# Attention and a gated MLP on one core: where the layernorm of later token blocks is placed, and how fill matmuls are dealt out among the others

## The chip, the cores and the metric

The kernel runs on one core of one Trainium2 chip. The metric is device time in microseconds (us) for one execution; smaller is better. The core has five engines that run side by side and meet only through semaphores: TensorE (PE in the profile, with its weight loads as PEld), VectorE (DVE), ScalarE (ACT), GpSimd (POOL) and SyncE (SP), which issues most DMA transfers here. In this kernel the order of instructions on every engine is fixed by the order of the program's text: an instruction whose input is late holds up everything behind it on the same engine.

## The reference

One launch computes an attention branch `s`, a gate `g` from an MLP, and their product on a residual. All inputs are bf16.

```python
x = A_x                                   # 1 x 2048 x 512
xn = (x - mean) / sqrt(var + 1e-5)        # layernorm over the 512 columns
# attention: 32 query heads, 8 key/value heads, head width 128, the last W = 512 cached rows
q = (xn @ wq)                             # 2048 x 4096 -> 32 heads
p = softmax(q @ k.T * 128 ** -0.5)        # 2048 x 512 per head
s = concat_heads(p @ v) @ wo              # 2048 x 4096 @ 4096 x 512
# gate
g = silu(silu(xn @ w1) @ w2)              # 512 -> 1792 -> 512
out = x + s * g
```

## The kernel before

The 2048 tokens are cut into four blocks of 512 (`NBLK = 4`, `BLKT = 4` tiles of 128 tokens each). After a start-up stage that makes the first half of block 0's MLP, the main loop has 128 steps: one step for each block and query head (`HQ = 32`), so steps 0 to 31 are block 0, 32 to 63 block 1, and so on. A step issues twelve matmuls of its own: four scores, four that make the query two steps ahead, and four for the value product of four steps ago (`LAG = 4`). Between these it puts "fill" matmuls that belong elsewhere: in block 0 the MLP of all four blocks (392 of them), in the later blocks the output projection of the block before (four a step). Every matmul of the loop is 128x128 weights on 512 columns.

```python
LAG = 4
PS_BUFS = {"sc": 4, "q": 1, "o": 1, "f": 2}      # PSUM banks: 4 for scores, 1, 1, and 2 for fill

def stats(b, j):                                  # layernorm statistics of tile j of block b
    st = work.tile([P, nc.vector.BN_STATS_DIM], FP32, name="st", bufs=4)
    nc.vector.bn_stats(out=st, in_=x_blk[b][:, j, :])
    nc.vector.bn_aggr(out=mv[:, b * BLKT + j, :], in_=st)

def rstd_of(t0, n): ...                           # (var + 1e-5) ** -0.5 on GpSimd

def center(b, j):                                 # x <- (x - mean) * rstd, in place
    nc.vector.tensor_scalar(out=x_blk[b][:, j, :], in0=x_blk[b][:, j, :], ...)

def flip_x(b, j):                                 # transposed by DMA into xnT, which the matmuls read
    nc.sync.dma_start_transpose(xnT[b][:, :, j * P : (j + 1) * P], x_blk[b][:, j, :])
```

The fill of block 0 is made of two kinds of group. A hidden group (`h_unit`) is four matmuls into one fill bank, then a tanh on ACT and a multiply on DVE that empty the bank; one block has 14 of them. An output group (`o_unit`) is 14 matmuls into one bank, then the same two operations; one block has four. The order of the fill is: output groups of block 0, then hidden and output groups of block 1, of block 2, of block 3.

```python
def h_unit(f, c):
    if c == 0:
        cur["ps"] = ps.tile([P, BLK], FP32, name="h_ps", tag="f", bufs=2)
    nc.tensor.matmul(cur["ps"], w1_sb[f // FH][:, c, ...], xnT[b][:, c, 0:BLK], ...)
    if c == ND - 1:                               # ND = 4
        nc.scalar.activation(th, cur["ps"], ACT.Tanh, scale=0.5)
        nc.vector.scalar_tensor_tensor(out=hT[b][f // 2][:, f % 2, :], in0=th, scalar=1.0,
                                       in1=cur["ps"], op0=ALU.add, op1=ALU.mult)
```

Own work of a step: `score(s, j)` is one matmul into a score bank and an exponential on ACT; `normalise(s, j0, j1)` is a reciprocal and two multiplies on DVE; `flip(s)` is one DMA transpose of the step's 128x2048 probabilities, issued by SP; `q_units` and `pv_units` each end in a copy from PSUM on DVE (`qT`, `oT`).

The start: the loads, and the main loop with its hand-set cuts.

```python
for j in range(2):
    nc.sync.dma_start(x_blk[0][0:HP4, j, :], x0v[0:HP4, j, :])       # HP4 = 64 rows
    nc.scalar.dma_start(x_blk[0][HP4:P, j, :], x0v[HP4:P, j, :])
NE = NEARLY * P                                                       # 512 columns
nc.sync.dma_start(w1_sb[0][:, :, 0:NE], w1v[:, :, 0:NE])
nc.scalar.dma_start(x_blk[0][:, 2:4, :], x0v[:, 2:4, :])
nc.sync.dma_start(w1_sb[0][:, :, NE:], w1v[:, :, NE : FH * P])        # FH * P = 896 columns
nc.sync.dma_start(w1_sb[1], w1v[:, :, FH * P :])
nc.sync.dma_start(w2_sb[0], w2v[:, 0:FH, :])
load_x(1)
load_kq(0)
# ... w2_sb[1], further keys, queries' weights and values, load_x(2), load_x(3)

# start-up stage, block 0: statistics and centring of tiles 0 and 1, ten warm-up matmuls,
# transposes on PE, then 14 pairs of hidden groups, 256 columns at a time
for i in range(2 * FH):
    h_pair(i, i // FH)            # pair i: hidden columns f = 2*(i%7), 2*(i%7)+1; f >= 7 reads w1_sb[1]
    if i == 3:                    # transposes of tiles 2 and 3, and their copies to xnT[0] (ACT, DVE)
        ...
    # ... stats(1, .), and the queries of steps 0 and 1

def spread(n):
    cut = [n // 6] * 6
    for k in (5, 4, 1, 3, 0, 2)[: n % 6]:
        cut[k] += 1
    return cut if n != 4 else (0, 0, 0, 0, 2, 2)

for s in range(NSTEP):
    b, h = divmod(s, HQ)
    n = 4
    if b == 0:
        n = min(4 * (h + 1), n_more) + (h + 1) * (n_mlp - n_more) // HQ - done   # n_more = 16, n_mlp = 392
    cut = spread(n)
    qu = q_units(s + 2) if s + 2 < NSTEP else []
    pu = pv_units(s - LAG) if s >= LAG else []
    score(s, 0)
    if s >= 1:
        normalise(s - 1, 2, 3); flip(s - 1)
    for u in qu[:2]: u()
    pump(cut[0])                                  # pump(n): the next n fill matmuls
    for u in qu[2:]: u()
    pump(cut[1])
    score(s, 1)
    for u in pu[:2]: u()
    pump(cut[2])
    for u in pu[2:]: u()
    pump(cut[3])
    score(s, 2)
    normalise(s, 0, 1)
    pump(cut[4])
    score(s, 3)
    pump(cut[5])
    for b2, s0 in ((2, 2), (3, 8)):               # one tile's statistics a step: block 2 in 2 to 5, 3 in 8 to 11
        if s0 <= s < s0 + BLKT: stats(b2, s - s0)
        if s == s0 + BLKT - 1: rstd_of(b2 * BLKT, BLKT)
    if s < 2:
        for j in (2 * s, 2 * s + 1): center(1, j); flip_x(1, j)
    for b2, s0 in ((2, 7), (3, 14)):              # one tile centred and transposed a step: 7 to 10, 14 to 17
        if s0 <= s < s0 + BLKT: center(b2, s - s0); flip_x(b2, s - s0)
    # ... loads of later keys, values and weights
```

From step 27 on `wo` is loaded, and after the last step a tail multiplies block 3 out with fewer products; neither is touched.

Of the kernel before, what the change touches and what calls it, by code (L numbers as in the profile page):

```python
# [9 lines left out]
P = 128  # L10
# [6 lines left out]
LAG = 4  # L17
# [5 lines left out]
def kernel(  # L23
# [12 lines left out]
    nc = tc.nc  # L36
# [10 lines left out]
    BLKT = 4  # L47
# [3 lines left out]
    NSTEP = NBLK * HQ  # L51
    FH = NFC // 2
    HALF = BLK // 2
    HP = HQ // 2
    HP4 = P // 2
# [28 lines left out]
    w1_sb = [reg.tile([P, ND, FH * P], BF16, name=f"w1_{i}", tag=f"big{i}") for i in range(2)]  # L84
# [8 lines left out]
    x_blk = {}  # L93
# [13 lines left out]
    def stats(b, j):  # L107
# [4 lines that stand above are left out]
    def rstd_of(t0, n):  # L112
        v = rstd[:, t0 : t0 + n]
        nc.gpsimd.tensor_scalar_add(v, mv[:, t0 : t0 + n, 1], 1e-5)
        nc.gpsimd.tensor_tensor(out=v, in0=v, in1=neg_half[:, 0:n], op=ALU.pow)
# [5 lines left out]
    def center(b, j):  # L121
        t = b * BLKT + j
        nc.vector.tensor_scalar(
            out=x_blk[b][:, j, :],
            in0=x_blk[b][:, j, :],
            scalar1=mv[:, t, 0:1],
            scalar2=rstd[:, t : t + 1],
            op0=ALU.subtract,
            op1=ALU.mult,
        )  # L130

    def flip_x(b, j):
        nc.sync.dma_start_transpose(xnT[b][:, :, j * P : (j + 1) * P], x_blk[b][:, j, :])

    def load_kq(g):
        nc.sync.dma_start_transpose(
            kT[g].rearrange("p (o w) -> p o w", o=1), A_k_cache[0, g, ds(SK - W, W), :]
        )
        nc.sync.dma_start(wq_sb[g], wqv[:, :, g * REP * DH : (g + 1) * REP * DH])

    def load_v(g):
        nc.sync.dma_start(
            v_sb[g], A_v_cache[0, g, ds(SK - W, W), :].rearrange("(c p) d -> p c d", p=P)
        )
# [82 lines left out]
    def score(s, j):  # L227
        h = s % HQ
        if j == 0:
            p_all[s] = work.tile([P, NKC, BLKT, P], BF16, name="p_all", tag="p_all", bufs=4)  # L230
            den[s] = work.tile([P, BLKT], FP32, name="den", bufs=3)
        sc = ps.tile([P, W], FP32, name="sc_ps", tag="sc", bufs=4)
        nc.tensor.matmul(  # L233
            sc, qT[s][:, j * P : (j + 1) * P], kT[h // REP], start=True, stop=True
        )
        nc.scalar.activation(  # L236
            p_all[s][:, :, j, :],
            sc.rearrange("p (kc q) -> p kc q", q=P),
            ACT.Exp,
            scale=INV_SQRT_DH,  # L240
            accum_out=den[s][:, j : j + 1],
        )

    def normalise(s, j0, j1):
        rden = work.tile([P, 2], FP32, name="rden", bufs=4)
        nc.vector.reciprocal(rden, den[s][:, j0 : j1 + 1])  # L246
        for j in range(j0, j1 + 1):
            nc.vector.tensor_scalar_mul(  # L248
                p_all[s][:, :, j, :], p_all[s][:, :, j, :], rden[:, j - j0 : j - j0 + 1]
            )  # L250

    def flip(s):
        pT[s] = work.tile([P, NKC, BLK], BF16, name="pT", tag="pT", bufs=4)
        nc.sync.dma_start_transpose(
            pT[s].rearrange("p kc (j q) -> p (kc j) q", q=P), p_all[s][:, :, :, :]
        )
# [47 lines left out]
    def new_wo(tag):  # L304
        wo_tiles[tag] = reg.tile([P, len(WO_HOME[tag]), D], BF16, name=f"wo_{tag}", tag=tag)
# [20 lines left out]
    def out_units(b):  # L326
        acc = {}
        xes = {}

        def mm(j, h):  # L330
            t = b * BLKT + j
            if h == 0:
                acc[j] = ps.tile([P, D], FP32, name="s_ps", tag="f", bufs=2)
            nc.tensor.matmul(  # L334
                acc[j],
                oT[(b * HQ + h) // 2][:, h % 2, j * P : (j + 1) * P],
                wo_of(h),
                start=(h == 0),
                stop=(h == HQ - 1),
            )  # L340
            if h == HQ // 2:
                xes[j] = reg.tile([P, D], BF16, name="x_e", tag=f"pair{4 + j % 2}")
                nc.gpsimd.dma_start(xes[j], x2[ds(t * P, P), :])
            if h == HQ - 1:
                xe = xes[j]
                sg = reg.tile([P, D], FP32, name="sg", tag=f"pair{2 + j % 2}")
                nc.vector.tensor_tensor(out=sg, in0=acc[j], in1=g_sb[b][:, j, :], op=ALU.mult)
                nc.vector.scalar_tensor_tensor(
                    out=xe, in0=sg, scalar=0.25, in1=xe, op0=ALU.mult, op1=ALU.add
                )  # L350
                nc.gpsimd.dma_start(out2[ds(t * P, P), :], xe)  # L351

        return [lambda a=a: mm(*a) for a in out_order()]
# [254 lines left out]
    w1v = B_w1.rearrange("(c p) f -> p c f", p=P)  # L608
# [5 lines left out]
    with tc.manual_schedule(engines={ENG.PE, ENG.Activation, ENG.DVE, ENG.SP, ENG.Pool}):  # L614
        new_x(0)
        x0v = x2[ds(0, BLK), :].rearrange("(j p) d -> p j d", p=P)
        for j in range(2):
            nc.sync.dma_start(x_blk[0][0:HP4, j, :], x0v[0:HP4, j, :])  # L618
            nc.scalar.dma_start(x_blk[0][HP4:P, j, :], x0v[HP4:P, j, :])
        NE = NEARLY * P  # L620
        nc.sync.dma_start(w1_sb[0][:, :, 0:NE], w1v[:, :, 0:NE])
        nc.scalar.dma_start(x_blk[0][:, 2:4, :], x0v[:, 2:4, :])
        nc.sync.dma_start(w1_sb[0][:, :, NE:], w1v[:, :, NE : FH * P])
        nc.sync.dma_start(w1_sb[1], w1v[:, :, FH * P :])
        nc.sync.dma_start(w2_sb[0], w2v[:, 0:FH, :])
        load_x(1)
        load_kq(0)
# [82 lines left out]
        for i in range(2 * FH):  # L710
# [8 lines left out]
            if i in (2 * FH - 3, 2 * FH - 2):  # L719
                k = i - 2 * FH + 3  # L720
# [11 lines left out]
        def pump(n):  # L732
            nonlocal done
            for _ in range(n):
                if fill:
                    fill.pop(0)()
                    done += 1
# [11 lines left out]
        }  # L749
        sums = col_sums()  # L750

        def spread(n):

            cut = [n // 6] * 6
            for k in (5, 4, 1, 3, 0, 2)[: n % 6]:
                cut[k] += 1
            return cut if n != 4 else (0, 0, 0, 0, 2, 2)

        n_more = 4 * LAG
        wo_first = False  # L760
        for s in range(NSTEP):
            b, h = divmod(s, HQ)
            if b >= 1 and h == 0:
                assert done >= n_mlp or b > 1
                fill += out_units(b - 1)
            n = 4
            if b == 0:
                n = min(4 * (h + 1), n_more) + (h + 1) * (n_mlp - n_more) // HQ - done
            cut = spread(n)
            qu = q_units(s + 2) if s + 2 < NSTEP else []  # L770
            pu = pv_units(s - LAG) if s >= LAG else []
            score(s, 0)
            if s >= 1:
                normalise(s - 1, 2, 3)
                flip(s - 1)
            for u in qu[:2]:
                u()
            pump(cut[0])
            for u in qu[2:]:
                u()  # L780
            pump(cut[1])
            score(s, 1)
            for u in pu[:2]:
                u()
            pump(cut[2])
            for u in pu[2:]:
                u()
            pump(cut[3])
            score(s, 2)
            normalise(s, 0, 1)  # L790
            pump(cut[4])
            score(s, 3)
            if s == NSTEP - 1:
                normalise(s, 2, 3)
                flip(s)
            pump(cut[5])
            while sums and sums[0][0] <= s:
                sums.pop(0)[1]()
            for b2, s0 in ((2, 2), (3, 8)):
                if s0 <= s < s0 + BLKT:  # L800
                    stats(b2, s - s0)
                if s == s0 + BLKT - 1:
                    rstd_of(b2 * BLKT, BLKT)
            if s < 2:
                for j in (2 * s, 2 * s + 1):
                    center(1, j)
                    flip_x(1, j)
            for b2, s0 in ((2, 7), (3, 14)):
                if s0 <= s < s0 + BLKT:
                    center(b2, s - s0)  # L810
                    flip_x(b2, s - s0)
            if s % REP == 1 and s < HQ and s // REP + 2 < HKV:
                load_kq(s // REP + 2)
                load_v(s // REP + 2)
            if not wo_first and done >= n_mlp - BLKT * NFC:
                new_wo("big0")
                new_wo("big1")
                wo_first = True
            if s == HQ:
                for tag in ("big2", "big3", "pair0", "pair1"):  # L820
                    new_wo(tag)
            for args in wo_plan.get(s, []):
                load_wo(*args)
# [29 lines left out]
```

The softmax here doesn't subtract the row's maximum and nothing guards it: scores larger than these inputs give would overflow.

## Time and profile before

| | |
|---|---|
| device time, median of 3 | 551.11 us (550.99 to 552.62) |
| span of the profiled execution | 548.9 us |
| granted TensorE clock | 1.00 |
| PE matmul busy | 542.9 us (99%) in 2676 matmuls |
| DVE busy | 458.3 us (83%) |
| ACT busy | 390.2 us (71%) |
| mean DMA traffic | 163 GB/s |
| loop steps of block 0 (first score of step 0 to that of step 32) | 22.16 to 187.69 us |
| loop steps of blocks 1 to 3 | 187.69 to 514.89 us |

In the profile, a line of the timeline gives the start in us, the duration in us, the engine, the line of the kernel, the operation, what it writes and reads (`out<-in`) and how many instructions were merged; in square brackets the idle time of that engine before it and what ended it. A busy time of PE is not PE at its peak, because a matmul's record is longer than the distance to the next one: the recorded matmuls of the loop take 380 ns each, and start 216 ns apart when nothing holds them up.

### The profile page before, as it was taken

What the parts mean: (1) busy time and instruction counts of PE and PEld (TensorE: products, weight loads), DVE (VectorE), ACT (ScalarE), POOL (GpSimd) and SP (SyncE); (2) the same over time, 40 slices, a digit from 0 to 9 for tenths busy, and PEclk for the clock granted to TensorE, in tenths of its full rate; (3) what the DMA queues carried; (4) which work ended last, traced back from release to release, by engine and by line L of the source; (5) the groups of instructions that cost most, each with busy time, mean ns of one, the idle gap of its engine ahead of it and who ended that gap; (6) DMA issues with size and microseconds to landing.
All of it is one profiled execution on the core that took longest, in us unless ns stands there. A gap on an engine that the chain in (4) does not pass through costs nothing.

```text
span 548.9 us, 8539 instructions
## 1 busy us (share of the span) xinstructions
PE 542.9 (99%) x2676; PEld 260.9 (48%) x2676; DVE 458.3 (83%) x1262; ACT 390.2 (71%) x1125; POOL 20.4 (4%) x41
## 2 busy tenths in 40 slices
PE   8999999999999999999999999999999999999997
PEld 5644444444444444444444444444444444444586
DVE  6869987976886688898888888988889889988897
ACT  5558756766776677777777777777788888888700
POOL 1000000000000100010001000100010000100010
PEclk9999999999999999999999999999999999999999
DMA  8968778768749799979887988797889887988831
GB/s 273 264 112 181 154 149 165 152 145 170 148 87 184 174 205 229 200 161 185 162 143 159 188 158 150 153 192 153 154 155 183 154 154 153 193 153 154 152 99 39
DMA packets 297869, 89.69 MB, mean 163 GB/s; under 512 B 282336, under 2 KB 296928, under 8 KB 297824
## 3 DMA queue, kind: packets, MB, share of 16 engines
q1 hardware_dynamic: 296080, 85.09, 78.6%
q0 software_dynamic: 1312, 3.67, 2.6%
q10 hardware_dynamic: 432, 0.39, 0.3%
q8 instruction: 21, 0.34, 0.2%
q14 instruction: 24, 0.20, 0.1%
HBM read 17.30 MB, written 2.10 MB: 35 GB/s over the span
## 4 chain that ended last, share of the span: by engine, by line
PE 96%; DMA 1%; DVE 1%; SPq 0%; ACT 0%; issue 0%
PE o_ps L276 20%; PE q_ps L211 20%; PE sc_ps L233 20%; PE s_ps L334 15%; PE oB_ps L180 9%; PE h_ps L147 6%; PE m_ps L477 4%; PE h_ps L697 2%; DMA w_1_112<-in_B_w_dram 1%; ACT th L157 0%; SPq L618 0%; DVE hT_4_1763 L158 0%; DVE gate_419 L190 0%; DVE hT_5_1764 L158 0%; DVE hT_2_1761 L158 0%
## 5 line engine op out<-in xcount | busy, mean ns | idle before, releaser
L236 ACT ACTIVATE p_all<-sc_ps 128x512 bf16<-128x512 f32 x512 | 305.4, 597 | 103.3 <-PE sc_ps L233 101.2
L248 DVE TENSOR_SCALAR p_all<-p_all,rden 128x512 bf16<-128x512 bf16 x512 | 158.0, 351 | 9.1
L282 DVE CAST oT<-o_ps 128x512 bf16<-128x512 f32 x128 | 88.3, 690 | 40.5 <-PE o_ps L276 39.6
L236 ACT ACTIVATION_READ_ACCUMULATOR p_all<-sc_ps 128x1 f32 x512 | 100.7, 197 | 0.0
L233 PEld LDWEIGHTS <-qT 128*128 128x128 bf16 x512 | 50.1, 98 | 61.4 <-issue 1.4
L223 DVE CAST qT<-q_ps 128x512 bf16<-128x512 f32 x111 | 76.3, 687 | 1.6 <-PE q_ps L211 1.5
L334 PEld LDWEIGHTS <-oT 128*128 128x128 bf16 x384 | 37.5, 98 | 45.3
L246 DVE RECIPROCAL rden<-den 128x2 f32<-128x2 f32 x256 | 40.5, 158 | 10.8 <-ACT p_all L236 10.8
L157 ACT ACTIVATE th<-h_ps 128x512 bf16<-128x512 f32 x42 | 25.1, 598 | 9.1 <-PE h_ps L147 9.1
L334 PE MATMUL s_ps<-wo_big_2086,oT 128*128 128x512 bf16 x84 | 26.0, 380 | 0.0
L334 PE MATMUL s_ps<-wo_big_2348,oT 128*128 128x512 bf16 x84 | 26.0, 380 | 0.0
L334 PE MATMUL s_ps<-wo_big_2087,oT 128*128 128x512 bf16 x84 | 26.0, 380 | 0.0
L334 PE MATMUL s_ps<-wo_big_2347,oT 128*128 128x512 bf16 x84 | 26.0, 380 | 0.0
L233 PE MATMUL sc_ps<-kT_91,qT 128*128 128x512 bf16 x64 | 24.3, 380 | 0.0
L233 PE MATMUL sc_ps<-kT_92,qT 128*128 128x512 bf16 x64 | 24.3, 379 | 0.0
L233 PE MATMUL sc_ps<-kT_93,qT 128*128 128x512 bf16 x64 | 24.3, 379 | 0.0
L233 PE MATMUL sc_ps<-kT_94,qT 128*128 128x512 bf16 x64 | 24.3, 379 | 0.0
L233 PE MATMUL sc_ps<-kT_96,qT 128*128 128x512 bf16 x64 | 24.3, 379 | 0.0
L233 PE MATMUL sc_ps<-kT_97,qT 128*128 128x512 bf16 x64 | 24.3, 379 | 0.0
L233 PE MATMUL sc_ps<-kT_95,qT 128*128 128x512 bf16 x64 | 24.3, 379 | 0.0
L233 PE MATMUL sc_ps<-kT_98,qT 128*128 128x512 bf16 x64 | 24.0, 379 | 0.0
L351 POOL DMA_DIRECT2D out_dram<-x_e x12 | 6.6, 549 | 313.6 <-DVE rden L246 257.3
(318 smaller groups left out, 831.3 us busy)
## 6 DMA issues: line engine op xcount, KB each, us to landing
pT<-p_all SPq DMA_TRANSPOSE x128, 4.4
x_e<-in_A_x_dram POOLq DMA_DIRECT2D x12, 128.0 KB, 2.9
out_dram<-x_e POOLq DMA_DIRECT2D x12, 128.0 KB, 2.2
w_1_112<-in_B_w_dram SPq DMA_DIRECT2D x1, 896.0 KB, 7.3
w_0_113<-in_B_w_dram SPq DMA_DIRECT2D x1, 896.0 KB, 9.4
w_1_114<-in_B_w_dram SPq DMA_DIRECT2D x1, 896.0 KB, 10.0
w_0_111<-in_B_w_dram SPq DMA_DIRECT2D x1, 512.0 KB, 4.9
x_129<-in_A_x_dram SPq DMA_DIRECT2D x1, 512.0 KB, 10.3
```

The lines of the kernel that those rows point to most:

```text
L147: nc.tensor.matmul(h_ps[:, lo : lo + n], w1_sb[f // FH][:, c, (f % FH) * P : (f % FH + 1) * P], xnT[b][:, c, lo : lo + n], start=(c == 0), ...
L157: nc.scalar.activation(th, h_ps, ACT.Tanh, scale=0.5)
L180: nc.tensor.matmul(cur["ps"], hT[b][f // 2][:, f % 2, j * P : (j + 1) * P], w2_sb[f // FH][:, f % FH, :], start=(f == 0), stop=(f == NFC - 1),
L211: nc.tensor.matmul(cur["ps"], wq_sb[h // REP][:, c, (h % REP) * DH : (h % REP + 1) * DH], xnT[b][:, c, :], start=(c == 0), stop=(c == ND - 1),
L223: nc.vector.tensor_copy(qT[s], cur["ps"])
L233: nc.tensor.matmul(sc, qT[s][:, j * P : (j + 1) * P], kT[h // REP], start=True, stop=True)
L236: nc.scalar.activation(p_all[s][:, :, j, :], sc.rearrange("p (kc q) -> p kc q", q=P), ACT.Exp, scale=INV_SQRT_DH, accum_out=den[s][:, j : ...
L246: nc.vector.reciprocal(rden, den[s][:, j0 : j1 + 1])
L248: nc.vector.tensor_scalar_mul(p_all[s][:, :, j, :], p_all[s][:, :, j, :], rden[:, j - j0 : j - j0 + 1])
L276: nc.tensor.matmul(cur["ps"], v_sb[h // REP][:, kc, :], pT[s][:, kc, :], start=(kc == 0), stop=(kc == NKC - 1))
L282: nc.vector.tensor_copy(oT[s // 2][:, s % 2, :], cur["ps"])
L334: nc.tensor.matmul(acc[j], oT[(b * HQ + h) // 2][:, h % 2, j * P : (j + 1) * P], wo_of(h), start=(h == 0), stop=(h == HQ - 1),)
```

## The change

It has three parts.

1. The layernorm of blocks 2 and 3 moves into steps in which the fill consists of output groups, where DVE has fewer banks to empty: block 2 gets its statistics in steps 8 and 9 and is centred and transposed in steps 10 and 11; block 3 gets statistics in steps 12, 18 and 19 and is centred and transposed in steps 20 and 21. Mostly two tiles are now treated in one step.
2. In block 0 the aim is an even distance between the fill groups, whose two banks ACT and DVE must empty in time: the six hand-set cuts go, and behind each of a step's own matmuls comes one fill matmul (in every fourth step one of them goes without; in the first four steps, which have no value product yet, there are up to two behind each). Blocks 1 to 3 keep their order.
3. In the start-up loads, the second half of `w1` comes in two pieces of 512 and 384 columns, so that its first columns can be waited for alone. Tile 1 of block 0's `x` is now one transfer on ACT's queue and no longer half on each queue, so that SP issues one transfer less ahead of `w1`.

```diff
-        for j in range(2):
-            nc.sync.dma_start(x_blk[0][0:HP4, j, :], x0v[0:HP4, j, :])
-            nc.scalar.dma_start(x_blk[0][HP4:P, j, :], x0v[HP4:P, j, :])
+        nc.sync.dma_start(x_blk[0][0:HP4, 0, :], x0v[0:HP4, 0, :])
+        nc.scalar.dma_start(x_blk[0][HP4:P, 0, :], x0v[HP4:P, 0, :])
+        nc.scalar.dma_start(x_blk[0][:, 1, :], x0v[:, 1, :])
 ...
-        nc.sync.dma_start(w1_sb[1], w1v[:, :, FH * P :])
+        nc.sync.dma_start(w1_sb[1][:, :, 0:NE], w1v[:, :, FH * P : FH * P + NE])
+        nc.sync.dma_start(w1_sb[1][:, :, NE:], w1v[:, :, FH * P + NE :])
 ...
+        def settle(b2, j):
+            center(b2, j)
+            flip_x(b2, j)
+
+        ln_plan = {
+            0: [(settle, 1, (0, 1))],
+            1: [(settle, 1, (2, 3))],
+            8: [(stats_of, 2, (0, 1))],
+            9: [(stats_of, 2, (2, 3))],
+            10: [(settle, 2, (0, 1))],
+            11: [(settle, 2, (2, 3))],
+            12: [(stats_of, 3, (0,))],
+            18: [(stats_of, 3, (1,))],
+            19: [(stats_of, 3, (2, 3))],
+            20: [(settle, 3, (0, 1))],
+            21: [(settle, 3, (2, 3))],
+        }
 ...
-            (score, normalise, flip, q, pv with pump(cut[0]) to pump(cut[5]) as above)
+            S = [lambda j=j: sc(j) for j in range(BLKT)]     # sc: score, with normalise and flip as before
+            if b == 0:
+                units = S[0:1] + qu + S[1:2] + pu[:2] + S[2:3] + pu[2:] + S[3:4]
+                for i, u in enumerate(units):
+                    u()
+                    pump((i + 1) * n // len(units) - i * n // len(units))
+            else:
+                for u in S[0:1] + qu + S[1:2] + pu + S[2:3]:
+                    u()
+                pump(2)
+                S[3]()
+                pump(2)
 ...
-            (the three loops for stats, center and flip_x at fixed steps)
+            for what, b2, js in ln_plan.get(s, ()):          # at the end of step s
+                for j in js:
+                    what(b2, j)
```

(`stats_of` is `stats`, and `rstd_of` after the block's last tile.)

More of the change, by code (lines that the diff above doesn't have):

```diff
@@ L750, with stats_of @@
         sums = col_sums()
[L752 to L757, printed above, removed]
-        n_more = 4 * LAG
+        n_more = 4 * LAG
+        def stats_of(b2, j):
+            stats(b2, j)
+            if j == BLKT - 1:
+                rstd_of(b2 * BLKT, BLKT)
+        def settle(b2, j):
[14 more added lines that the diff above has]
+        }
         wo_first = False
@@ L768 @@
                 n = min(4 * (h + 1), n_more) + (h + 1) * (n_mlp - n_more) // HQ - done
-            cut = spread(n)
             qu = q_units(s + 2) if s + 2 < NSTEP else []
             pu = pv_units(s - LAG) if s >= LAG else []
[L772 to L796, printed above, removed]
+            def sc(j):
+                score(s, j)
+                if j == 0 and s >= 1:
+                    normalise(s - 1, 2, 3)
+                    flip(s - 1)
+                if j == 2:
+                    normalise(s, 0, 1)
+                if j == 3 and s == NSTEP - 1:
+                    normalise(s, 2, 3)
+                    flip(s)
@@ L798 @@
                 sums.pop(0)[1]()
[L799 to L811, printed above, removed]
+            for what, b2, js in ln_plan.get(s, ()):
+                for j in js:
+                    what(b2, j)
```

## The prediction
> **What bounds the kernel now.** I read the page's first part, then PE's waits, then the stretches between stage borders, and then PE's own timeline where the stretches lose time.
>
> The page, busy time and share by engine:
>
> ```profile
> PE 542.9 (99%) x2676; PEld 260.9 (48%) x2676; DVE 458.3 (83%) x1262; ACT 390.2 (71%) x1125; POOL 20.4 (4%) x41
> ```
>
> PE is the bound. But 99% doesn't say how much is left, so the second view is five stretches of the span (start-up before the first hidden matmul, start-up stage, block 0, blocks 1 to 3, tail):
>
> ```profile
> 0.00:7.32 7.32, 5.41 (x20) 1.89 (x21) 3.80 (x15) 3.00 (x6) 0.71 (x7) 1.00 0.67 198
> 7.32:22.16 14.84, 14.59 (x129) 11.97 (x129) 12.66 (x26) 9.04 (x16) 0.95 (x2) 1.00 1.15 305
> 22.16:187.69 165.53, 165.04 (x762) 74.25 (x761) 132.10 (x341) 111.55 (x313) 4.60 (x7) 1.00 0.77 156
> 187.69:514.89 327.20, 327.20 (x1517) 148.25 (x1516) 280.44 (x808) 262.32 (x779) 11.54 (x22) 1.00 0.87 168
> ```
>
> The counts in brackets include one or two matmuls that straddle a border, so I take the program's. Blocks 1 to 3 up to that border have 94 steps of 16 matmuls and one of 12, 1516: 327.20 / 1516 = 0.2158 us each. Their steps are all 3.45 us long, with no gap at all; nothing can be won there and the change leaves their order alone. Block 0 has 32 steps: 128 scores, 128 for queries, 112 for values, 392 fill, 760 in all. At 0.2158 us that is 164.0 us, and it takes 165.53. **So block 0 loses 1.5 us to stalls**, and that is all that parts 1 and 2 can win.
>
> Where the 1.5 us sits, PE's waits do not tell; they list three, all in the start-up:
>
> ```profile
> PE warm_ps L639 <- DVE eps L74: 1.2, 1, 1.2
> PE t_ps L646 <- DVE x_119 L654: 0.7, 1, 0.7
> PE h_ps L697 <- DMA w_1_112<-in_B_w_dram: 0.2, 1, 0.2
> ```
>
> A stall under 164 ns is hidden in the 380 ns of a record, and a longer one is shown with that taken off. So one looks at starts. PE, 149.3 to 151.3 us (step 24, hidden groups of block 3), and DVE beside it:
>
> ```profile
> 150.18 0.38 PE L233 MATMUL sc_ps<-kT_97,qT 128*128 128x512 bf16 x1
> 150.40 0.38 PE L147 MATMUL h_ps<-xnT_110,w_0_111 128*128 128x512 bf16 x1
> 150.89 0.38 PE L147 MATMUL h_ps<-xnT_110,w_1_112 128*128 128x512 bf16 x1
> ```
>
> ```profile
> 149.30 0.69 DVE L282 CAST oT<-o_ps 128x512 bf16<-128x512 f32 x1 [0.18 <-PE o_ps L276]
> 150.15 0.69 DVE L158 SCALAR_TENSOR_TENSOR hT_2_1761<-th,h_ps 128x512 bf16<-128x512 bf16 x1 [0.15 <-ACT th L157]
> ```
>
> From 150.40 to 150.89 is 0.49 us in place of 0.22. The matmul at 150.89 opens a new hidden group and needs the bank that DVE empties from 150.15 to 150.84. The same 0.27 us returns at 155.85 and 161.30, and comes also at 41.81; smaller ones (0.06 to 0.20) stand at 56.32, 103.25, 110.21 and 113.86. All are at hidden groups; together they are the 1.5 us.
>
> **What the Trainium skill says.** "Perfetto Trace Analysis", section Identifying the Most-Contended Engine, says that matmul busy time is no measure of how near PE is to its peak. This trace agrees: records of 380 ns at a distance of 216. "TensorE: Matmul & The Clock Gate", section Back-to-back issue gap, gives N / 2.4 + 2.5 ns for an isolated warm matmul, 215.8 ns at 512 columns, and about 131 ns sustained; the trace has 215.8 sustained, so the first figure is the floor here. "Perfetto Trace Analysis", section Optimization Strategy, says that a gap that keeps returning can mean too few buffers; here that is the two fill banks. "DMA: Bandwidth & Descriptors", section Issuing engines are not separate DMA queues, says that transfers from different engines share the same 16 DMA engines and interleave; I use it for the start.
>
> **Part 3, the start.** What it removes: at 10.27 us PE waits for the second half of `w1`.
>
> ```profile
> 9.28 1.25 PE L697 MATMUL h_ps<-xnT_107,w_0_111 128*128 128x256 bf16 x10
> 10.79 0.61 PE L697 MATMUL h_ps<-xnT_107,w_1_112 128*128 128x256 bf16 x4 [0.25 <-DMA w_1_112<-in_B_w_dram]
> ```
>
> Ten matmuls at 0.109 us from 9.28 end their issue at 10.37, so 0.41 us is lost. The half is 896 KB, lands 7.3 us after its issue at 3.42, and the stretch from 7.32 to 22.16 above moves 305 GB/s. With 512 KB to wait for, the first piece is in 393 KB (384 x 1024 bytes) / 305 = 1.3 us earlier, at about 9.5: the wait goes. The second piece lands where the whole landed, and pair 5 needs it only 2 us later. Not all 0.41 us stays won: pair 7 needs the copy of tile 3 to `xnT`, which DVE makes from 13.46 to 13.88 in a chain that hangs on GpSimd's power at 10.2 us and not on PE. PE reaches pair 7 at 14.30 now and could at 13.89. I book **-0.35 us**.
>
> What it moves: the statistics of tile 1 wait 0.20 us for x now, at 4.45, and everything on DVE up to the first hidden matmul follows. The tile now comes whole on ACT's queue and shares the DMA engines with a `w1` piece issued 0.85 us earlier. It may land 0.2 us sooner or 0.4 later: **0 +- 0.3**.
>
> **Part 2, one behind each.** A hidden group is four fill matmuls. With the old cuts (twelve fills in a step of 24) three groups take 9, 10 and 6 places or so, and the shortest distance between the last matmul of a group and the first of the next but one, which needs its bank, is 8 places, 1.73 us. The chain to be done in it is the matmul's 0.38, tanh 0.60, multiply 0.69, semaphores about 0.1: 1.77 with no queueing. That is the 0.27 stall once queueing is added. With one behind each the distance is always 10 places, 2.16 us, which leaves 0.39 for queueing. Laying a step out by hand with an exponential taking 0.59 of ACT and the DVE work in its order (multiplies 0.6, qT and oT 0.6 each, two normalises of 0.73), each of the four alignments a step can have just fits, by 0.13 us in the tightest. DVE has 4.5 us of work in such a step of 5.18. I expect most but not all of the 1.5 us gone: **-1.2 us**.
>
> **Part 1, the layernorm.** It adds and removes no instruction; a tile's statistics cost DVE about 0.8 us (records of 0.69 and 0.18) and its centring 0.33 to 0.41. A step with output groups leaves DVE 2.0 us free (5.2 less 0.6 for qT, 0.6 for oT, 1.5 for the normalises and 0.5 for 0.8 of a gate multiply), so two statistics fit; in a step of hidden groups, with 0.7 free, even one did not. The saving is counted in part 2. **The new cost is lateness.** Fill 168 is the first matmul on block 2's `xnT`: the first fill of step 13. Fill 280 is the first on block 3's: the seventh fill of step 22, at place 13, 13 x 0.216 = 2.8 us into the step. The matmul reads all 512 columns, so it needs all four DMA transposes. The last two are emitted at the end of step 21. Their pace is seen at steps 0 and 1, where block 1 is settled in the same way; SP's own timeline:
>
> ```profile
> 28.93 2.53 SPq L133 DMA_TRANSPOSE xnT_108<-x_129  x2
> 31.55 2.52 SPq L254 DMA_TRANSPOSE pT<-p_all  x1
> 34.17 2.96 SPq L133 DMA_TRANSPOSE xnT_108<-x_129  x2
> ```
>
> and the line's landing times:
>
> ```profile
> DMA to landing us min/median/max: 2.4/2.4/4.0
> ```
>
> Step 22 by the clock from its start: the last value matmul of step 21 is at place 20, 4.3 us into a step of 5.2; DVE's copy starts 0.4 later and takes 0.6, so the centring runs from 0.2 to 0.9 after the border (first tile ready at 0.6). SP issues at 0.6 and 1.9, and the second lands 2.4 later: 4.3. The probability transpose of step 20 lies ahead in the same queue (issued about 3.1 us into step 21, behind the first pair, landing 4.4 later, at about 2.3 of step 22), and can push this to 4.6 or 5. Against 2.8 that is a stall of 1.5 to 2.2 us; I book **+1.7 us**, once. For block 2 the same reckoning, with a gate multiply ahead of oT in step 11, gives the last landing at 5.2 to 5.4 us into step 12, and the need at 5.2: **+0.1 us**.
>
> **Sum:** -0.35 + 0 - 1.2 + 1.7 + 0.1 = +0.25; 551.1 + 0.25, about **551.3 us**.
>
> **Rivals.** (a) The transposes of block 3 come in time, because DVE runs less far behind or SP issues sooner: then -1.5, 549.6 us. For it: all single landings but a few took 2.4. Against: the first issue cannot precede the centring, and two issues and a landing alone are 3.7 us. (b) Even spacing brings small stalls at every one of 42 hidden groups, since the margin is 0.13 us: 0.05 each is 2 us, and 553 us with the late transpose. Against: DVE idles 14% of such a step. (c) The x load is held up by `w1`: +0.4 at the start, 551.7. (d) The stall is longer, with the probability transpose in SP's way for its whole issue of 2.5 to 3.4 us: 552 to 552.5.
>
> **Range and chances.** Everything the change touches is a gain of at most 0.4 + 1.5 us and a stall of some 2 us; 2% is 11 us. Range 550.0 to 552.5. Faster by over 2%: 0.01; within: 0.98; slower: 0.01.
>
> **What would show it.** Right: no gap at 10.3 us; block 0's hidden groups at 0.216 throughout; one gap of 1.5 to 2 us on PE in step 22, ended by a transpose of `xnT` of block 3; step 13 with none or a small one; steps from 32 on 3.45 us. Wrong: step 22 without a gap (rival a), or returning gaps of 0.05 to 0.3 at hidden groups (b), or the first hidden matmul later than 7.4 us (c).

## The result and the profile after

The changed kernel takes 553.56 us (median of 6 runs, 553.25 to 556.47) against 551.10 for the kernel before, measured beside it: ratio 1.0052, 95% interval 1.0028 to 1.0075. It is slower, by half a percent, and lies above the range that was predicted (550.0 to 552.5).

The same stretches as before, with their borders at the same events (first hidden matmul, first score of step 0, of step 32, of step 127); in the third the span goes up from 165.53 to 167.89 us, in the fourth nothing changes:

```profile
0.00:7.47 7.47, 5.22 (x21) 1.81 (x21) 4.18 (x16) 3.50 (x6) 0.72 (x7) 1.00 0.67 198
7.47:21.89 14.42, 14.37 (x127) 12.10 (x129) 12.21 (x25) 8.54 (x16) 0.96 (x2) 1.00 1.17 292
21.89:189.78 167.89, 163.91 (x747) 74.25 (x761) 132.60 (x341) 113.29 (x313) 5.27 (x8) 1.00 0.77 155
189.78:516.99 327.21, 325.63 (x1488) 148.34 (x1517) 280.61 (x809) 262.50 (x779) 11.17 (x21) 1.00 0.88 168
```

(48 of the 2676 matmul records are missing from this trace, so its PE counts and busy times are not to be compared with those before; the program issues as many matmuls as it did.)

PE's waits, all five:

```profile
PE h_ps L147 <- DMA xnT_110<-x_139: 2.1, 1, 2.1
PE warm_ps L640 <- DVE eps L74: 1.2, 1, 1.2
PE h_ps L147 <- DMA xnT_109<-x_137: 1.0, 1, 1.0
PE t_ps L647 <- DVE x_119 L655: 0.6, 1, 0.6
PE h_ps L698 <- DMA w_0_111<-in_B_w_dram: 0.5, 1, 0.5
```

Two waits are new in block 0, both for transposed `x`: of block 3 (first line) and of block 2 (third). The wait for the second half of `w1` has gone, and one for its first piece has come. PE's timeline at the two new places:

```profile
138.76 0.38 PE L276 MATMUL o_ps<-pT,v_103 128*128 128x512 bf16 x1
141.21 0.39 PE L147 MATMUL h_ps<-xnT_110,w_0_111 128*128 128x512 bf16 x1 [2.06 <-DMA xnT_110<-x_139]
```

```profile
88.65 0.38 PE L233 MATMUL sc_ps<-kT_94,qT 128*128 128x512 bf16 x1
90.03 0.38 PE L147 MATMUL h_ps<-xnT_109,w_0_111 128*128 128x512 bf16 x1 [0.99 <-DMA xnT_109<-x_137]
```

Start to start these are 2.44 and 1.37 us where 0.216 is due: 2.23 us lost in step 22 and 1.16 in step 13. Of the old losses at hidden groups two are left, 0.28 (41.33 us) and 0.18 (112.47), so 0.46 of 1.50. The first score of step 0 comes 0.27 us earlier. Together: 2.23 + 1.16 - 1.04 - 0.27 = 2.08 us, and the two profiled spans, 548.9 and 551.0, differ by 2.1. The profile is accounted for; the medians differ by 2.46. The rest, 0.4 us, was not profiled; two of the six runs lie at 554.94 and 556.47 us, and spreads of that kind came from the start where one was profiled (below).

### The profile page after: what moved, and what is told of

Same layout as the page of the kernel before. It is cut to its first block, busy times and chain, and to the rows that moved or that the text cites. A ratio compares the mean times of both kernels' runs of the same rounds, so it can differ in the third digit from the quotient of the medians.

```text
span 551.0 us, 8493 instructions
## 1 busy us (share of the span) xinstructions
PE 539.7 (98%) x2628; PEld 261.1 (47%) x2676; DVE 458.9 (83%) x1262; ACT 392.1 (71%) x1125; POOL 20.7 (4%) x41
## 4 chain that ended last, share of the span: by engine, by line
PE 94%; DMA 2%; DVE 1%; issue 1%; ACT 0%; SPq 0%
PE sc_ps L233 20%; PE q_ps L211 19%; PE o_ps L276 19%; PE s_ps L334 15%; PE oB_ps L180 8%; PE h_ps L147 6%; PE m_ps L477 4%; PE h_ps L698 2%; DMA w_0_111<-in_B_w_dram 1%; DMA xnT_109<-x_137 1%; DMA xnT_110<-x_139 1%; DVE p_all L248 0%; DVE oT L282 0%; ACT th L189 0%; DVE gate_416 L190 0%
## 5 line engine op out<-in xcount | busy, mean ns | idle before, releaser
L334 PE MATMUL s_ps<-wo_big_2348,oT 128*128 128x512 bf16 x82 | 25.5, 379 | 0.1
L334 PE MATMUL s_ps<-wo_big_2087,oT 128*128 128x512 bf16 x82 | 25.5, 379 | 0.1
L334 PE MATMUL s_ps<-wo_big_2347,oT 128*128 128x512 bf16 x82 | 25.5, 379 | 0.1
L334 PE MATMUL s_ps<-wo_big_2086,oT 128*128 128x512 bf16 x81 | 25.3, 379 | 0.2
L276 PE MATMUL o_ps<-pT,v_104 128*128 128x512 bf16 x63 | 18.3, 379 | 0.2
```

Of the source, the lines that this page charges most:

```text
L276: nc.tensor.matmul(cur["ps"], v_sb[h // REP][:, kc, :], pT[s][:, kc, :], start=(kc == 0), stop=(kc == NKC - 1))
L334: nc.tensor.matmul(acc[j], oT[(b * HQ + h) // 2][:, h % 2, j * P : (j + 1) * P], wo_of(h), start=(h == 0), stop=(h == HQ - 1),)
```

## The experiments

Each kernel was run beside the kernel before on the same chip, each series on another chip; the kernel before had medians of 551.20 (first series of four kernels), 551.18 (second, three) and 551.10 (third, three).

### What each part does alone

**The old layernorm steps in the changed kernel** (parts 2 and 3 without 1).

```diff
-            8: [(stats_of, 2, (0, 1))],  9: [(stats_of, 2, (2, 3))],
-            10: [(settle, 2, (0, 1))],  11: [(settle, 2, (2, 3))],  12: ... 21: ...
+            2 to 5: one (stats_of, 2, j) a step;   7 to 10: one (settle, 2, j) a step
+            8 to 11: one (stats_of, 3, j) a step;  14 to 17: one (settle, 3, j) a step
```

> The changed kernel with the layernorm of blocks 2 and 3 put back into its old steps (statistics in 2 to 5 and 8 to 11, centring in 7 to 10 and 14 to 17, one tile a step); even fill and new loads stay. Theory (late transposes cost 1.2 us in step 13 and 2.2 us in step 22, everything else in the change is a small gain): both gaps vanish, some 0.2 to 0.6 us of small stalls at hidden groups come back where statistics fall into steps 3 to 5 and centring into 14 to 17; about 550.6 us, ratio to before 0.999. Rival (even spacing itself is what costs): stays at 553 us or more.

Measured 552.03 us, ratio 1.0022 (1.0012 to 1.0033), with 4 of 16 runs at 554.1 to 554.6. Both waits for a transpose are gone, as the theory said. But the rest is not a small gain: PE's waits show DVE's multiply of hidden groups in their place.

```profile
PE warm_ps L640 <- DVE eps L74: 1.2, 1, 1.2
PE h_ps L147 <- DVE hT L158: 1.1, 3, 0.5
PE h_ps L698 <- DMA w<-in_B_w_dram: 0.7, 1, 0.7
```

Gaps of 0.27, 0.32, 0.62, 0.66, 0.29 and 0.22 us add to 2.4 where the old cuts lost 1.5. DVE's timeline at the third shows why:

```profile
49.33 0.68 DVE L109 BATCH_NORM_STATS2 st<-x 128x6 f32<-128x512 bf16 x1
50.05 0.18 DVE L110 BATCH_NORM_AGGREGATE mv<-st 128x2 f32<-128x6 f32 x1
50.15 0.13 DVE L246 RECIPROCAL rden<-den 128x2 f32<-128x2 f32 x1
50.31 0.62 DVE L248 TENSOR_SCALAR p_all<-p_all,rden 128x512 bf16<-128x512 bf16 x2
50.84 0.68 DVE L158 SCALAR_TENSOR_TENSOR hT<-th,h_ps 128x512 bf16<-128x512 bf16 x1
```

A statistic of block 2 (49.33) and a normalise stand ahead of the multiply that empties the bank (50.84 to 51.52), and PE goes on at 51.58.

**Even fill alone**: the kernel before with the one-behind-each loop, old steps and old loads.

> The kernel before with part 2 alone: one fill matmul behind each own one, old layernorm steps, old loads. With the new loads and the old layernorm steps block 0 lost 2.2 us at hidden groups (before 1.5 us), in steps 3 to 6 and 17, where statistics and centring share DVE with hidden groups. Theory (even spacing pays only when the layernorm is out of those steps): 551.2 + 0.6 = 551.8 us. Rival (that loss came from the new loads' shifted start): 551.2 us or less.

Measured 551.99 us, ratio 1.0013 (1.0007 to 1.0020); the theory's 551.8 is nearly met. Its block 0 takes 188.61 - 22.21 = 166.40 us against 165.53. Even spacing on its own makes the kernel slower. It does take away the three gaps of 0.27 us at block 3's hidden groups, but in steps 4 to 6, where block 2's statistics stand, it loses 0.32, 0.62 and 0.66 us where the old cuts lost 0.09. Why the old cuts lost so little there, with the same statistics in the same steps, stays open.

**The layernorm steps alone**: the kernel before with the new plan, old cuts, old loads.

> The kernel before with part 1 alone: new layernorm steps, old cuts, old loads. With the old cuts the first matmul on block 2's transposed x stands two places later in step 13 and that of block 3 three places later in step 22, so 0.43 and 0.65 us of the two gaps are hidden. Theory: gaps of about 0.7 and 1.6 us, less some 0.5 us of hidden-group stalls that the layernorm had caused; about 552.5 us. Rival (even spacing costs): no loss, 551.1 us or less.

Measured 553.14 us, ratio 1.0032 (1.0020 to 1.0044). The direction is right, the parts are not: block 3's transposes cost 1.35 us, block 2's nothing, and the hidden groups lose 1.7 us, no less than before (three of the 0.27 us gaps stand in block 3's groups, where no layernorm ever was). Moving the layernorm away doesn't help while the cuts bunch the groups. That block 3's transposes cost something and block 2's nothing fits the instruction fetches below: the last transpose of block 3 met one here and took 3.2 us to land, the last of block 2 met none while its data moved and took 2.5.

**The loads alone**, in two series.

> The kernel before with part 3 alone. Theory: the wait for the second half of w1 is gone, but the first piece of w1 now shares the DMA engines with tiles 2 and 3 of x and lands 0.2 to 0.5 us later, so the gain is 0.1 to 0.3 us in most runs (median 551.0 us); and in some of the runs tile 1 of x, on ACT's queue, is overtaken by the first w1 piece and lands 2 to 3 us late, which puts a tail of runs at 553 to 555 us. Rival (the slow starts seen with one layernorm plan are chance and not of the loads): all runs within 0.5 us of the median.

> Part 3 alone once more, in one series with the two runs beside it. Open: slow starts (553 us and more) came in 4 of 16, 4 of 22 and 4 of 16 runs of three kernels with the new loads, and in 0 of 13 of the new loads alone, in another series. Theory (the race of tile 1 of x with the first w1 piece): in this series the two kernels with new loads have such a tail or both have none, whatever their layernorm plan, and the one with old x loads has none. Rival (the tail belongs to the plan): it comes with the early layernorms and not here.

Measured 551.15 us, ratio 1.0001 (0.9992 to 1.0009), with all of 13 runs from 550.8 to 551.7; and in the other series 551.61, ratio 1.0012 (0.9998 to 1.0027), with five of 14 runs from 552.6 to 554.3 (one more took 1494 us, and one of the kernel before 1173; the ratio leaves both out). So the tail, the runs some 2 to 4 us above the others, is not in every series, and where it is, it is there with no layernorm moved. The profile of the second is one of those runs, and its PE waits for the first piece of `w1`:

```profile
6.85 0.38 PE L640 MATMUL warm_ps<-warm 128*128 128x512 bf16 x1
8.96 1.34 PE L698 MATMUL h_ps<-xnT,w 128*128 128x256 bf16 x7 [1.73 <-DMA w<-in_B_w_dram]
```

The piece was issued at 1.37 us and landed at 8.91; in the kernel before it was issued at 2.24 and landed at 7.16. Tiles 2 and 3 of `x`, on ACT's queue, landed at 8.70 (5.24 before). Two transfers that move together were both late, which fits the theory that they hold each other up but doesn't show it apart from other causes; that it is tile 1 of `x` which loses doesn't hold here, it landed at 3.75.

### The late transposes

**Both layernorms one step earlier**, everything else as changed, in two series.

```diff
+            2: [(stats_of, 2, (0, 1))],
+            8: [(stats_of, 2, (2, 3))],
+            9: [(settle, 2, (0, 1))],
+            10: [(settle, 2, (2, 3))],
+            11: [(stats_of, 3, (0,))],
+            12: [(stats_of, 3, (1,))],
+            18: [(stats_of, 3, (2, 3))],
+            19: [(settle, 3, (0, 1))],
+            20: [(settle, 3, (2, 3))],
```

> The changed kernel with both layernorms one step earlier, still in steps of output groups: block 2 statistics in 2 and 8, centring in 9 and 10; block 3 statistics in 11, 12 and 18, centring in 19 and 20. The last transposes land about 5 to 6 us into steps 11 and 21, a whole step before they are read. Theory: no gap in steps 13 and 22, hidden groups as even as in the changed kernel; 553.6 - 3.4 = 550.2 us, faster than before by 0.9 us. Rival (the transposes' place is not the cause): 553 us.

> The layernorms one step early with the new loads, once more. Theory: median 550.5 us, and a tail above 552.5 us if and only if the new loads alone have one in this series. Rival: a tail here alone.

Measured 550.63 us, ratio 0.9998 (0.9989 to 1.0008), and 550.72, ratio 1.0006 (0.9991 to 1.0020). No wait for a transpose is left in either. Most runs lie at 550.1 to 551.3, about where the theory put the kernel (550.2), but 4 of 22 and 7 of 22 at 552.8 to 554.7, and with them the gain can't be told from nothing. The profile of the first is one of these; here tile 1 of `x` did lose the race (issued at 1.33, landed at 6.33), DVE's statistics waited, and PE's timeline shows what follows:

```profile
4.14 1.49 PE L640 MATMUL warm_ps<-warm 128*128 128x512 bf16 x3
7.75 0.65 PE L647 MATMUL t_ps<-ident,x 128*128 128x128 bf16 x4 [2.12 <-DVE x L655]
```

**Instruction fetches moved.** In the changed kernel the last transpose of each block took 3.4 and 3.1 us to land, and their neighbours 2.4. The DMA view of two stretches tells the difference. First the next to last pair's second transpose of block 3 (132.87 to 135.31 us, from issue to landing), then the last (138.06 to 141.16):

```profile
q1 hardware_dynamic: 1045, 0.25, 51.6%
issues: line engine op xcount, KB each, median us to landing
xnT_110<-x_139 SPq DMA_TRANSPOSE x1, 2.4
```

```profile
q1 hardware_dynamic: 1311, 0.32, 49.9%
q14 instruction: 1, 0.01, 1.0%
issues: line engine op xcount, KB each, median us to landing
...
xnT_110<-x_139 SPq DMA_TRANSPOSE x1, 3.1
```

The second stretch holds one transfer of queue 14, 8 KB of instructions, from 139.86 to 140.36 us, just as the transpose's data moves. To move it, tiny instructions were put where their engines idle:

```diff
+    shift = const.tile([P, 1], FP32, name="shift")
+    for _ in range(10):
+        nc.vector.memset(shift, 0.0)
 ...
+            if i == 1:
+                for _ in range(8):
+                    nc.scalar.copy(scratch, scratch)
```

> The changed kernel with ten empty memsets of one column on VectorE before the first statistics and eight copies of one column on ScalarE while it waits at 10 us, which cost nothing where they stand. They move the places at which these two engines fetch their next 8 KB of instructions by about 4 us to the front of the same work. In the changed kernel an instruction fetch of 0.3 and 0.5 us stands in the data phase of each of the two late transposes (88.3 and 139.9 us), which landed 3.4 and 3.1 us after issue where their neighbours took 2.4. Theory (the fetch holds them up): both land after 2.4 to 2.5 us, gaps 0.2 and 1.6 us, 552.0 us. Rival (they are late because another transpose is queued before and behind them): gaps as before, 1.2 and 2.2 us, 553.5 us.

Measured 552.32 us, ratio 1.0028 (1.0017 to 1.0039), with two of 16 runs at 555.5. The last transposes now land 2.43 and 2.46 us after issue. PE at steps 13 and 22:

```profile
88.48 0.38 PE L236 MATMUL sc_ps<-kT,qT 128*128 128x512 bf16 x1
88.90 0.38 PE L150 MATMUL h_ps<-xnT,w 128*128 128x512 bf16 x1
```

```profile
137.82 0.38 PE L279 MATMUL o_ps<-pT,v 128*128 128x512 bf16 x1
139.62 0.39 PE L150 MATMUL h_ps<-xnT,w 128*128 128x512 bf16 x1 [1.43 <-DMA xnT<-x]
```

The gaps are 0.21 and 1.59 us, as this theory expected (0.2 and 1.6) and not as its rival did (1.2 and 2.2). The fetch now falls at 137.27, when the last transpose has been issued but moves nothing yet; it met the first of the pair, which took 3.0 us to land and ends no wait. Over the twelve kernels profiled here (before and after too) `xnT` was written by 144 transposes; 43 of them landed more than 2.8 us after issue, and every one of the 43 had a fetch (queue 14, 8 KB, or queue 8, 16 KB) between issue and landing. Of the other 101, 24 had one; of the 77 that met none, the slowest took 2.74 us.

### A version that is faster than both

The layernorms one step earlier, even fill, the second half of `w1` in two pieces, and tile 1 of `x` in halves on both queues as before; in two series.

```diff
-        nc.scalar.dma_start(x_blk[0][:, 1, :], x0v[:, 1, :])
+        nc.sync.dma_start(x_blk[0][0:HP4, 1, :], x0v[0:HP4, 1, :])
+        nc.scalar.dma_start(x_blk[0][HP4:P, 1, :], x0v[HP4:P, 1, :])
```

> The changed kernel with the layernorms one step earlier (as in the run of that name), the second half of w1 in two pieces, but tile 1 of x loaded in halves on both queues again, as before. Theory: no late transposes, even hidden groups (0.5 to 0.9 us lost of 1.5), no wait for w1 at 10 us, and no tail of slow starts: 551.2 - 0.6 - 0.35 = 550.2 us, all runs within 0.5 us; faster than before by a ratio of about 0.998. Rival (the slow starts come from the split of w1 and not from x): a tail at 553 us or more stays.

> The layernorms one step early with x loaded as before, once more. Both theories: 550.5 us, all runs within 0.5 us of it, no tail; faster than before by 0.6 us.

Measured 550.54 us, ratio 0.9989 (0.9982 to 0.9995), and 550.51, ratio 0.9988 (0.9982 to 0.9995); all 43 runs lie between 550.3 and 551.5. The tail is gone, in the third series beside two kernels that have it (5 of 14 and 7 of 22 runs; the kernel before had one such run in 50, of 553.8). So it belongs to the order of the first loads, and not to the layernorm plan nor to the second half of `w1` in two pieces, which this version keeps. What it gives up is tile 1 of `x` on ACT's queue together with the earlier issue of `w1` (1.37 us and not 2.24); these two were not tried apart. The stretches up to step 127:

```profile
0.00:7.23 7.23, 5.71 (x20) 1.93 (x21) 3.80 (x15) 3.00 (x6) 0.71 (x7) 1.00 0.66 194
7.23:21.72 14.49, 14.43 (x128) 11.97 (x129) 12.56 (x26) 9.03 (x16) 0.95 (x2) 1.00 1.15 300
21.72:186.65 164.93, 163.74 (x748) 74.35 (x762) 132.41 (x341) 113.17 (x313) 4.94 (x8) 1.00 0.80 158
```

Block 0 is at 164.93 us, 0.9 above its floor of 164.0, and the start is 0.44 us shorter. PE's last matmul starts 1.04 us before that of the kernel before (544.24 and 545.28); of this the span shows 0.6. In the profile of the second series, of a run of 551.02 us, block 0 takes 164.94 us too, but the start is only 0.12 us shorter. The time from the last landing to the end of the program was 1.3 us and not 0.9 in both profiles of this version; why was not tried.

## Why the prediction was wrong, point by point

| term | booked, us | measured, us |
|---|---|---|
| start | -0.35 | -0.27 |
| hidden groups, even fill with the layernorm out of the way | -1.2 | -1.04 (in part luck, see below) |
| block 2's transposes, step 13 | +0.1 | +1.16 |
| block 3's transposes, step 22 | +1.7 | +2.23 |
| sum | +0.25 | +2.08 |

**The bound, the floor and the mechanism were right.** PE's distance of 0.216 us, the 1.5 us that could be won, the steps from 32 on unchanged, and a new wait in step 22 that a transpose of `xnT` ends, are all in the profile. DVE and SP ran as reckoned: the centring of block 3's last tiles begins 0.17 us into step 22 (136.34, step 22 starting at 136.17) against 0.2, and SP issues 0.60 and 1.89 into it against 0.6 and 1.9.

```profile
136.34 0.73 DVE L123 TENSOR_SCALAR x_139<-x_139,mv,rstd 128x512 bf16<-128x512 bf16 x2
```

**The step that failed is the landing**: "the second lands 2.4 later", in both blocks. Measured it was 3.4 us for block 2 and 3.1 for block 3. With the 2.4 to 2.5 us that the run with moved fetches restored, the two terms are 0.21 and 1.59, near the booked 0.1 and 1.7; so 1.6 of the 1.8 us by which the sum was off is this term. The quoted line itself, 2.4/2.4/4.0, held the warning: its maximum was passed over ("all single landings but a few took 2.4"), and the few were not looked up. In the kernel before the transposes at 34.17, 82.45 and 116.36 took 3.1, 4.0 and 3.3 us, each with a fetch in it, and no one waited for them.

**A reason was wrong inside a right number.** Step 22's arrival was put at up to 5 us into the step, because step 20's probability transpose lay ahead in the queue. The arrival was 4.99, but that transpose had landed at 138.61 and the first of the pair came through at 2.45 us; what delayed the second was the fetch. Rival (d), SP held up for the whole of an issue, didn't happen.

**The saving was credited to one part and belongs to two.** The -1.2 was booked to even fill, with the layernorm's share "counted in part 2". The two runs of single parts show +0.8 us for even fill alone and no gain at hidden groups for the layernorm steps alone; only both together take the hidden groups from 1.5 us to 0.5, or to 0.9 where no transpose is late. Rival (b), small stalls at every group, is refuted: with both parts two gaps are left in 42 groups.

Part of the 1.04 is luck. With the layernorms one step earlier, where no transpose is late, a third gap stands in step 13 (here in the version with the old `x` loads):

```profile
91.99 0.38 PE L233 MATMUL sc_ps<-kT,qT 128*128 128x512 bf16 x1
92.58 0.38 PE L147 MATMUL h_ps<-xnT,w 128*128 128x512 bf16 x1 [0.21 <-DVE hT L158]
```

It costs 0.38 us; with the fetches moved, after a wait of 0.21 us in the same step, it costs 0.18; in the changed kernel, after 1.16 us, it is not there. This fits a late transpose that hides a loss at a hidden group. Without late transposes 0.90 us is left (0.34, 0.38 and 0.18), a gain of 0.6 and not of 1.04 or 1.2.

**The start** gained near what was said, by a different route. Tile 1 of `x` came early (its statistics start at 4.14 us, not 4.45), but the first `w1` piece landed at 7.42 and not 7.16 although it was issued 0.86 us sooner, and PE waited for it (0.5 us in the list of waits). The first piece of the second half landed at 10.14 and not at about 9.5, still 0.4 us before it was read. That the spread of runs would grow was not foreseen; rival (c) named the right place, the first loads, with a fixed 0.4 us in place of 0 to 4. That sharing the DMA engines is what delays them is argued here, not shown.

## What to carry to other kernels

When work is moved to a stage with a free engine, reckon when its result is first read, through every queue to the landing, and take the worst landing of the profile and not the median when the slack is under a microsecond. A stall that needs two things cured (a bunched order and a loaded engine) pays nothing, or costs, while only one is cured; test changes in pairs as well as alone. Look at the spread of the runs and not only at the median: the new order of the first loads left the median nearly as it was and, in two of three series, put some runs 2 to 4 us higher.

## What the hardware showed unexpectedly

Instruction fetches get in the way of data transfers. Most 128x512 transposes landed 2.4 us after issue; the 43 late ones took 2.9 to 4.4 us, each with a fetch of 8 KB (0.3 to 0.8 us) or 16 KB (0.9 to 1.3 us) in between. Which transpose is met depends on how many instructions an engine has run: eighteen tiny ones, placed at no cost, moved among others the fetch at 139.86 to 137.27 us and took 1.6 us of stall away at the two late transposes (1.4 net of the gap of 0.18 us above).

A large part of what a late start costs in the tail runs is PE's clock. In every profile the first warm-up matmuls, of 512 columns, start 0.43 us apart, twice the loop's 0.216. The trace's first record of the full clock comes at 4.1 to 7.1 us in eleven profiles, and at 13.34 in that of one step early, first series; until then its hidden matmuls of 256 columns start 0.213 us apart, later 0.109. (The profile's granted clock reads 1.00 in this stretch too, but the trace has no clock record there.) In the profile of the loads alone, second series, the trace records half the clock from 9.35 to 12.76 us:

```profile
9.35:12.76 3.41, 3.41 (x18) 2.42 (x17) 2.18 (x7) 1.10 (x2) 0.95 (x2) 0.50 1.10 343
12.76:16.17 3.41, 3.41 (x37) 3.10 (x36) 2.52 (x5) 2.28 (x5) 0.00 (x0) 1.00 1.43 183
```

Half of the matmuls stand in the first stretch. Against the profile of the first of its two series the first hidden matmul comes 0.93 us later (8.96 and 8.03), the first score 2.60 later (25.05 and 22.45), and the run takes 2.63 us more. So 1.67 of it falls behind that first matmul, and half of the 3.41 us at half clock is 1.7. Of the 20 tail runs of the old steps, the loads alone and the two series of one step early, 13 have a mean recorded clock of 0.996 or 0.997; of the 53 others none is below 0.998.

Between the first warm-up and the first hidden matmul PE idled up to 2.12 and 1.73 us at a time in these two starts, and 1.08 at most in the other ten. But after 2.06 us of idle time in step 22 of the changed kernel the matmuls went on 0.216 us apart, so when an idle time costs clock stays open.
